# Key-value sums with the value columns as weights, 256 feature columns moving, and the normaliser summed on VectorE

## The chip, the cores and the metric

The kernel runs on one core of a Trainium2 chip. The metric is the device time of one execution in microseconds; the time of a kernel is the median of its runs. The engines are named as in the profile: PE (TensorE matmuls) and PEld (its weight loads), DVE (VectorE), ACT (ScalarE), POOL (GpSimd), SP (SyncE, which here only issues DMAs). Every line number "L12" is a line of the kernel's file.

## The reference

Two branches over the same input x (2048 tokens, width 1024) are mixed by a gate per token:

```python
g = sigmoid((x * gate_w).sum(-1))
a = linear_attention(x)          # 32 heads of width 32
b = (gelu(x @ w_gate) * (x @ w_up)) @ w_down
return g * a + (1 - g) * b
```

The attention branch maps queries and keys of each head by a learned matrix and two softmaxes, and replaces the square attention matrix by two sums over all tokens:

```python
phi = lambda t: concat([softmax(t @ w_phi), softmax(-(t @ w_phi))])   # 64 features a head
kv = einsum("bhsf,bhsd->bhfd", phi(k), v)      # sums over the 2048 tokens s
z  = einsum("bhsf->bhf", phi(k))               # the normaliser
o  = (phi(q) @ kv) / (phi(q) @ z + 1e-6)
return o @ wo
```

The change concerns kv and z only.

## The kernel before, in words

All large products (q, k, v, gate, up, and at the end the two output products) are computed with seven block products in the place of eight, in fp32 split into a high and a low part, so that a product of 128 x 512 outputs over 512 inputs is 12 matmuls (`product`, L703 to L709). The first phase is a list of 79 **units**, one for each pair of weight tiles of one half of the tokens: value and key units of the second half, then of the first half, then the first half's gate, up and query units, then the second half's (`units`, L294 to L299). A unit is seven products of 12 matmuls. The second phase (L1286 on) multiplies the results with `wo` and `w_down`.

Beside the units run **background jobs** that need PE only now and then. One kind makes the features of the keys and the key-value sums (`features`, L952): 32 jobs, one for each token half, each group of four heads, and each half of a group. A job reads a 64-row piece of k and v from memory, transposes it in blocks of 32 x 32 on DVE, takes maximum and minimum, the two exponentials on ACT, the sums and the division on DVE, and leaves the features in `pts` as a high and a low part, and the values in `blocks` likewise. Then PE adds up, over eight blocks of tokens, the products of features and values in a PSUM tile of the tag `misc` (`accumulate`, L1008). Before the change each block's features are the weights, first the high part with 130 moving columns (the values' high part, two columns of ones and zeros that give the normaliser, the values' low part), then the low part with 66: 16 matmuls a job (L1014). ACT copies four corners and the normaliser's column from PSUM (L1026, L1030), and GpSimd stores them with five DMAs (L1032, L1035).

When all 32 are stored, `finish` (L1039) loads the sums of both halves with four DMAs, adds them on DVE, turns the normaliser, and stores both for the **attention jobs** (`attention`, L1074), which then run in two places at once; `second_place` (L1189) opens the second one. Half way, at product 329 (`second_turn`), the operand x of PE is exchanged for that of the second half (`switch`, L259); the switch is due 13 products earlier, and uses buffers of the feature jobs (`switch_again`, L875). A feature job is not begun later than five or six products before that (L834, L974). The main background loop (L825) does an event that is due first, then `finish` when all sums are stored, then a further job.

The order of the instructions on PE, DVE, ACT and SP is written out when the kernel is built, by a planner (`run`, `emit`, `step`, L171 to L205 and L748). Each job is a generator that yields requests: engine, duration in microseconds, time from which it can run, and the product by which it is due. The planner keeps its own clock for each engine (a product is 2.73 us, `PRODUCT`), takes of those that can start the one due first, and fixes the order on each engine. PE work of the background goes to `fillers` and is put behind the next product after its operands are planned to be ready, with a length of its own (1.12 us for L1014). Feature requests are due three products after they are made. On the chip every engine keeps this order and waits only where data or buffers are not ready. GpSimd's queue carries all stores and, in the second half, the loads of kept weights (`kept_weights`, L375).

What the planner books on DVE can be read off the requests: weights of a unit 1.25 + 1.5 + 1.25 + 1.5 + 1.25 + 0.72 (L328 to L369); results of a gate unit 2 x 0.75 and of an up unit 2 x 1.47 + 2 x 0.75 (L675, L680); a feature job 0.72 + 0.72 + 1.4 + 0.72 + 1.4 + 1.6 + 1.25 + 1.25 (L968 to L1001).

Of the kernel before, what the change touches and what calls it, by code (L numbers as in the profile page):

```python
# [8 lines left out]
F32 = mybir.dt.float32  # L9
F32R = mybir.dt.float32r  # L10
# [21 lines left out]
def tile_gated_mix(ctx: ExitStack, tc: tile.TileContext, x, xT, wkT, wqT, wv, w_phi, wo,  # L32
# [15 lines left out]
    sign = keep.tile([P, 1], F32, name="sign")  # L48
# [8 lines left out]
    kv_parts = [dram.tile([P, H // 2, 64], F32, name=f"kvp{h}") for h in range(2)]  # L57
# [77 lines left out]
    with tc.tile_pool(name="xa", bufs=1) as xa, tc.tile_pool(name="fp", bufs=1) as fp, \  # L135
# [268 lines left out]
        V_BLOCK = P + 2  # L404

        def new_f(dtype):
            return fp.tile([P, 8 * V_BLOCK], dtype, tag="f", name="f", bufs=1)

# [60 lines left out]
        for j in range(4):  # L469
            nc.vector.memset(sign[32 * j:32 * j + 32], 1.0 - 2 * (j % 2))  # L470
        bd = fp.tile([P, NG, 4, 32], F32, tag="v", name="bd", bufs=1)
# [335 lines left out]
        places = [Place(work[:, 2048:3072], dict(mm=tails[:, :32], st=tails[:, 32:64], own=tails[:, 64:129]))]  # L807
# [38 lines left out]
        def first_part():  # L846
# [9 lines left out]
            yield VEC, 0.1, 0.0, now[0] + 6  # L856
            places[0].blocks = new_f(F32R).rearrange("p (b c) -> p b c", c=V_BLOCK)
# [25 lines left out]
        def gates(into, gw, free):  # L883
# [22 lines left out]
            for h in range(4):  # L906
                for q in range(4):
                    nc.vector.tensor_copy(g_at[32 * h:32 * h + 32, :, q], g_a[32 * q:32 * q + 32, :])
# [43 lines left out]
        def features(p, events):  # L952
# [6 lines left out]
            v = [blocks[:, :, c:c + 64].rearrange("p b (h d) -> p b h d", h=2) for c in (0, 66)]  # L959
# [6 lines left out]
            while job:  # L966
# [39 lines left out]
        v_free = [0.0]  # L1006

        def accumulate(half, pair, pts, blocks):  # L1008

            def emit_products(end):  # L1010
                po = misc()
                for b in range(8):
                    for a, n in ((0, V_BLOCK), (1, 66)):
                        nc.tensor.matmul(po[:, :n], pts[:, b, a].rearrange("p q f -> p (q f)"), blocks[:, b, :n],  # L1014
                                         start=b == a == 0, stop=b == 7 and a == 1, skip_group_check=True)
                misc_free[0] = INF
                pts_free[0] = v_free[0] = end
                start(accumulated(half, pair, po, end + 0.25))
            return emit_products

        def accumulated(half, pair, po, end):
            end = yield SCA, 1.1, end, now[0] + 2
            own = places[0].parts["own"]
            for h in range(2):
                for s in range(2):
                    nc.scalar.activation(  # L1026
                        own[64 * h + 32 * s:64 * h + 32 * s + 32, :64].rearrange("p (a d) -> p a d", a=2),
                        po[64 * s + 32 * h:64 * s + 32 * h + 32, :132].rearrange("p (a d) -> p a d", a=2)
                        [:, :, 32 * h:32 * h + 32], AF.Copy)
            nc.scalar.activation(own[:, 64:], po[:, 64:65], AF.Copy)  # L1030
            misc_free[0] = end
            nc.gpsimd.dma_start(kv_parts[half][:, pair], own[:, :64])  # L1032
            for s in range(2):
                for h in range(2):
# [454 lines left out]
```

## Time and profile before

| | |
|---|---|
| median of 3 runs | 2400.91 us (2397.92 to 2403.98) |
| the profiled execution | 2408.64 us, its span 2406.9 us |
| granted clock in it | 0.996 |
| PE busy | 2364.8 us, 98% of the span |
| DVE, ACT, POOL busy | 1767.3, 1117.5, 386.2 us |
| the 32 sets of L1014 | from 288.4 to 946.1 us |
| end of the first phase | 1717.2 us |

The profile is of one execution. Busy time of an engine is the union of its instructions. A group's row gives the line, engine, operation, what is written and read, the shape and count, then busy time and mean duration in ns, then the idle time before. A row of the timeline gives the start and the duration in us and, in brackets, how long the engine stood idle before it and for whom. A row of busy time by stretch gives for every engine its busy time and its count of instructions, then PE's granted clock, the DMA's busy share and its rate in GB/s. Matmuls are pipelined and their ends are modelled, so that the distance of two starts says more than a matmul's own duration.

### The profile page before, as it was taken

To read this page: it belongs to the slowest core of one execution; us is meant where nothing else is said; L and a number is where in the kernel's file an instruction comes from. 1 tells how busy PE (TensorE), PEld (TensorE's weight loads), DVE (VectorE), ACT (ScalarE), POOL (GpSimd) and SP (SyncE) were. 2 spreads that over 40 slices of the span, in tenths; PEclk is the share of its full clock that TensorE was granted. 3 is DMA by queue.
4 is the path that set the end of the run, shared out by engine and by line. 5 is a ranking of instruction groups with operands and counts; after the bars stand their busy time and mean duration, and the time that the engine had idled before them with its cause. 6 is when DMAs were issued, how large, how long until landed. Compare 5 with 4: busy or idle time off the path is not lost.

```text
span 2406.9 us, 30176 instructions
## 1 busy us (share of the span) xinstructions
PE 2364.8 (98%) x10664; PEld 1950.6 (81%) x10664; DVE 1767.3 (73%) x2369; ACT 1117.5 (46%) x1588; POOL 386.2 (16%) x721
## 2 busy tenths in 40 slices
PE   9999999999999999999999999999999999999999
PEld 7778888888888888877777788788888888888887
DVE  6667687888888886567968888894474778777773
ACT  5336455566555565344554565564344222323221
POOL 3201122222222223211112111111000000000000
PEclk9999999999999999999999999999999999999999
DMA  9878548888888878987787778787685667978774
GB/s 334 293 256 307 180 155 278 287 301 290 296 295 298 293 274 306 337 304 221 240 252 237 249 246 253 248 255 263 226 299 196 241 220 265 318 267 314 256 270 139
DMA packets 221046, 635.27 MB, mean 264 GB/s; under 512 B 34912, under 2 KB 70496, under 8 KB 196320
## 3 DMA queue, kind: packets, MB, share of 16 engines
q1 hardware_dynamic: 153312, 316.88, 40.8%
q0 software_dynamic: 66384, 316.21, 37.2%
q8 instruction: 84, 1.38, 0.2%
q14 instruction: 66, 0.54, 0.1%
q10 hardware_dynamic: 1200, 0.26, 0.1%
HBM read 426.13 MB, written 207.11 MB: 263 GB/s over the span
## 4 chain that ended last, share of the span: by engine, by line
PE 80%; DMA 7%; issue 7%; DVE 4%; POOL 1%; ACT 1%; SPq 0%; POOLq 0%; DVEq 0%; ACTq 0%
PE po L1400 28%; PE a L708 20%; PE c L708 14%; PE b L708 7%; PE p L708 6%; PE misc L1014 2%; DMA x<-sums 1%; DMA x<-q 1%; PE misc L1162 1%; DMA x<-in_xT 1%; DMA x<-xs 1%; DMA tyz<-rg5z 0%; DMA xs<-raw 0%; PE misc L929 0%; DMA tails<-sums 0%
## 5 line engine op out<-in xcount | busy, mean ns | idle before, releaser
L1400 PE MATMUL po<-tw,wgu 128*128 128x512 f32 x1344 | 309.8, 389 | 0.0
L1400 PEld LDWEIGHTS po<-tw,wgu 128*128 128x128 f32 x1344 | 252.3, 188 | 52.4
L118 ACT ACTIVATE wgu<-stage 128x1024 fp32r<-128x1024 f32 x131 | 138.9, 1060 | 295.9 <-PE po L1400 231.7
L708 PE MATMUL a<-s,tyz 128*128 128x512 f32 x948 | 239.0, 402 | 17.0 <-DMA tyz<-rg3z 3.7
L121 DVE TENSOR_TENSOR wgu<-stage,wgu 128x1024 fp32r<-128x1024 f32 x131 | 159.6, 1218 | 113.5 <-ACT wgu L118 113.3
L708 PE MATMUL p<-s,tyz 128*128 128x512 f32 x948 | 230.8, 392 | 3.8 <-ACT x L746 3.7
L708 PE MATMUL a<-s,v 128*128 128x512 f32 x948 | 234.2, 396 | 0.0
L708 PE MATMUL a<-x,wgu 128*128 128x512 f32 x948 | 229.0, 390 | 4.5 <-DVE x L676 3.7
L708 PE MATMUL b<-s,tyz 128*128 128x512 f32 x948 | 229.0, 390 | 3.9 <-ACT b L736 3.9
L708 PE MATMUL c<-x,wgu 128*128 128x512 f32 x948 | 230.3, 392 | 0.3 <-ACT c L729 0.3
L708 PE MATMUL c<-x,tyz 128*128 128x512 f32 x948 | 228.6, 390 | 1.3 <-ACT c L725 1.3
L708 PEld LDWEIGHTS a<-s,tyz 128*128 128x128 f32 x948 | 178.7, 192 | 60.4 <-issue 16.5
L708 PEld LDWEIGHTS p<-s,tyz 128*128 128x128 f32 x948 | 177.8, 189 | 43.3 <-ACT x L746 6.2
L708 PEld LDWEIGHTS a<-s,v 128*128 128x128 f32 x948 | 178.6, 188 | 42.1
L708 PEld LDWEIGHTS a<-x,wgu 128*128 128x128 f32 x948 | 177.3, 188 | 43.4 <-DVE x L676 4.5
L708 PEld LDWEIGHTS b<-s,tyz 128*128 128x128 f32 x948 | 177.2, 188 | 41.8 <-ACT b L736 5.1
L708 PEld LDWEIGHTS c<-x,wgu 128*128 128x128 f32 x948 | 177.8, 188 | 40.6 <-ACT c L729 0.7
L708 PEld LDWEIGHTS c<-x,tyz 128*128 128x128 f32 x948 | 178.1, 188 | 39.3 <-ACT c L725 2.1
L1400 PE MATMUL po<-tw,wl 128*128 128x512 f32 x672 | 156.9, 389 | 0.0
L1400 PE MATMUL po<-tyz,wgu 128*128 128x512 f32 x672 | 155.2, 389 | 0.0
L1400 PEld LDWEIGHTS po<-tw,wl 128*128 128x128 f32 x672 | 126.1, 188 | 26.2
L1400 PEld LDWEIGHTS po<-tyz,wgu 128*128 128x128 f32 x672 | 126.1, 188 | 26.2
(442 smaller groups left out, 3584.9 us busy)
## 6 DMA issues: line engine op xcount, KB each, us to landing
stage<-lm SPq DMA_DIRECT2D x98, 512.0 KB, 3.6
sr<-in_w_down SPq DMA_DIRECT2D x84, 512.0 KB, 5.7
sl<-lm SPq DMA_DIRECT2D x70, 512.0 KB, 4.4
lm<-h POOLq DMA_DIRECT2D x112, 256.0 KB, 4.5
stage<-in_w_gate SPq DMA_DIRECT2D x28, 512.0 KB, 4.9
stage<-in_w_up SPq DMA_DIRECT2D x28, 512.0 KB, 4.8
stage<-la SPq DMA_DIRECT2D x28, 512.0 KB, 4.1
sr<-in_wo SPq DMA_DIRECT2D x20, 512.0 KB, 5.9
```

Source lines behind the costliest of these rows:

```text
L118: nc.scalar.activation(dst, src, AF.Copy)
L121: nc.vector.tensor_tensor(dst, src, dst_h.bitcast(F32), OP.subtract)
L708: nc.tensor.matmul(dst, w[:, h, 4 * part + kc, :], xq[:, e, kc, :], start=first and kc == 0 and i == 0, stop=kc == 3 and i == 2, skip_grou ...
L1014: nc.tensor.matmul(po[:, :n], pts[:, b, a].rearrange("p q f -> p (q f)"), blocks[:, b, :n], start=b == a == 0, stop=b == 7 and a == 1, ski ...
L1162: nc.tensor.matmul(po[s], kbs[:, s].rearrange("p a b -> p (a b)"), pts[:, q, s, :], start=q == 0, stop=q == 1)
L1400: nc.tensor.matmul(ps[c], ls[:, a, m, c * P:(c + 1) * P], rs[:, e, m], start=opens and m == 0 and j == 0, stop=closes and m == 1 and j == 2)
```

## The change

The roles of the two operands of the key-value product are exchanged. The values' high and low part of a block (2 x 64 columns) are the weights, and the features' high and low part (2 x 128 columns) move, so there are 8 matmuls of 256 columns. A ninth, in plain fp32, with one moving column of ones, sums the normaliser over the partitions, after DVE has summed the features over the eight blocks in a new reduction in `features`. The two halves of the result are added on DVE out of PSUM into `own`; the store grows from 64 to 128 columns, and the normaliser goes with one store in the place of four. `finish` gets the sums with other axes, in pieces of 32 values, adds the two halves of partitions with a copy on ACT, and transposes. The places move: `own` and the normaliser lie in `tails`, the small places of the feature jobs in `g_at`, and so the copies into `g_at` are made at the end of `finish`.

```diff
-    sign = keep.tile([P, 1], F32, name="sign")
+    signs = keep.tile([P, 2], F32, name="sign")
+    sign, one = signs[:, :1], signs[:, 1:]
...
-    kv_parts = [dram.tile([P, H // 2, 64], F32, name=f"kvp{h}") for h in range(2)]
+    kv_parts = [dram.tile([P, H // 2, P], F32, name=f"kvp{h}") for h in range(2)]
...
-        places = [Place(work[:, 2048:3072], dict(mm=tails[:, :32], st=tails[:, 32:64], own=tails[:, 64:129]))]
+        places = [Place(work[:, 2048:3072], dict(
+            mm=g_at.rearrange("p c q -> p (c q)")[:, :32], st=g_at.rearrange("p c q -> p (c q)")[:, 32:],
+            own=tails[:, :P], z=tails[:, P:]))]
...
-            for half in range(2):
-                rows = slice(64 * half, 64 * half + 64)
-                nc.vector.tensor_copy(places[0].blocks[rows, :, 64:66],
-                                      pair_mask[rows, half, :16].rearrange("p (b c) -> p b c", c=2))
...
-            for h in range(4):
-                for q in range(4):
-                    nc.vector.tensor_copy(g_at[32 * h:32 * h + 32, :, q], g_a[32 * q:32 * q + 32, :])
...
                 high(pts[:, :, 0], by_block)
+                yield VEC, 1.25, z_free[0], soon()
+                z_free[0] = INF
+                nc.vector.tensor_reduce(p.parts["z"].rearrange("p (q f) -> p q f", q=4),
+                                        p.wide[0].rearrange("p (q b f) -> p q f b", q=4, f=32), AX.X, OP.add)
                 end = yield VEC, 1.25, end, soon()
                 low(pts[:, :, 1], by_block, pts[:, :, 0])
                 p.free = end
-                fillers.append((lambda end=end: max(end, misc_free[0]), accumulate(half, 2 * g + w, pts, blocks), 1.12))
+                fillers.append((lambda end=end: max(end, misc_free[0]), accumulate(half, 2 * g + w, pts, blocks), 1.1))
...
                 for b in range(8):
-                    for a, n in ((0, V_BLOCK), (1, 66)):
-                        nc.tensor.matmul(po[:, :n], pts[:, b, a].rearrange("p q f -> p (q f)"), blocks[:, b, :n],
-                                         start=b == a == 0, stop=b == 7 and a == 1, skip_group_check=True)
+                    nc.tensor.matmul(po[:, :2 * P], blocks[:, b], pts[:, b].rearrange("p e q f -> p (e q f)"),
+                                     start=b == 0, stop=b == 7, skip_group_check=True)
+                nc.tensor.matmul(po[:, 2 * P:2 * P + 1], places[0].parts["z"], one, start=True, stop=True,
+                                 skip_group_check=True)
...
         def accumulated(half, pair, po, end):
-            end = yield SCA, 1.1, end, now[0] + 2
...
-            misc_free[0] = end
-            nc.gpsimd.dma_start(kv_parts[half][:, pair], own[:, :64])
...
+            own, z = places[0].parts["own"], logit[:, pair:pair + 1]
+            end = yield VEC, 0.5, lambda end=end: max(end, own_free[0]), now[0] + 2
+            nc.vector.tensor_reduce(own, po[:, :2 * P].rearrange("p (e c) -> p c e", e=2), AX.X, OP.add)
+            nc.gpsimd.dma_start(kv_parts[half][:, pair], own)
+            own_free[0] = end + STORE
+            misc_free[0] = end = yield SCA, 0.25, end, now[0] + 2
+            nc.scalar.activation(z, po[:, 2 * P:2 * P + 1], AF.Copy)
+            nc.gpsimd.dma_start(z_parts[half][:, pair:pair + 1], z)
             kept.append(end + STORE)
...
         def finish(p):
             landed = yield SYN, LAND + 2.0, lambda: max(max(kept), place_free(), v_free[0]), INF
...
             for half in range(2):
-                nc.sync.dma_start(p.wide[half], kv_parts[half].rearrange("p u c -> p (u c)"))
-                nc.sync.dma_start(mm[:, half], z_parts[half])
+                for h in range(2):
+                    for k in range(2):
+                        rows = slice(64 * k + 32 * h, 64 * k + 32 * h + 32)
+                        nc.sync.dma_start(p.wide[half][rows].rearrange("p (u s f) -> p u s f", s=2, f=32),
+                                          kv_parts[half][rows].rearrange("p u (s h f) -> p u s h f", s=2, h=2)[:, :, :, h])
+                        nc.sync.dma_start(mm[64 * h + 32 * k:64 * h + 32 * k + 32, half],
+                                          z_parts[half][64 * k + 32 * h:64 * k + 32 * h + 32])
             soon = lambda: now[0] + 1
             end = yield VEC, 1.25, landed, soon()
             nc.vector.tensor_tensor(p.wide[0], p.wide[0], p.wide[1], OP.add)
...
+            moved = yield SCA, 1.1, end, soon()
+            nc.scalar.activation(p.wide[1][:64], p.wide[0][64:], AF.Copy)
+            yield VEC, 0.8, end - SIGNAL, soon()
...
+            end = yield VEC, 2.5, moved, soon()
+            nc.vector.tensor_tensor(p.wide[0][:64], p.wide[0][:64], p.wide[1][:64], OP.add)
+            nc.vector.transpose(p.wide[1][:64], p.wide[0][:64])
+            for h in range(2):
+                for s in range(2):
+                    nc.gpsimd.dma_start(sums_of[64 * h + 32 * s:64 * h + 32 * s + 32, 0],
+                                        p.wide[1][32 * h:32 * h + 32].rearrange("p (u s d) -> p s u d", s=2, d=32)[:, s])
+            yield VEC, 1.6, end - SIGNAL, soon()
+            for h in range(4):
+                for q in range(4):
+                    nc.vector.tensor_copy(g_at[32 * h:32 * h + 32, :, q], g_a[32 * q:32 * q + 32, :])
```

More of the change, by code (lines that the diff above doesn't have):

```diff
@@ L470, in tile_gated_mix @@
             nc.vector.memset(sign[32 * j:32 * j + 32], 1.0 - 2 * (j % 2))
+        nc.vector.memset(one, 1.0)
         bd = fp.tile([P, NG, 4, 32], F32, tag="v", name="bd", bufs=1)
@@ L855, in first_part @@
             pts_free[0] = max(folded[g] for g in range(NG))
-            yield VEC, 0.1, 0.0, now[0] + 6
-            places[0].blocks = new_f(F32R).rearrange("p (b c) -> p b c", c=V_BLOCK)
-            for half in range(2):
-                rows = slice(64 * half, 64 * half + 64)
-                nc.vector.tensor_copy(places[0].blocks[rows, :, 64:66],
-                                      pair_mask[rows, half, :16].rearrange("p (b c) -> p b c", c=2))
+            places[0].blocks = new_f(F32R).rearrange("p (b c) -> p b c", c=P)
             prepared[0] = 0.0
@@ L958, in features @@
             blocks = p.blocks
-            v = [blocks[:, :, c:c + 64].rearrange("p b (h d) -> p b h d", h=2) for c in (0, 66)]
+            v = [blocks[:, :, c:c + 64].rearrange("p b (h d) -> p b h d", h=2) for c in (0, 64)]
             v_now = p.e[:, 0].rearrange("p (h b d) -> p b h d", h=2, d=32)
@@ L1021, in accumulated @@
         def accumulated(half, pair, po, end):
-            end = yield SCA, 1.1, end, now[0] + 2
[L1023 to L1029, printed above, removed]
@@ L1030, in accumulated @@
-            nc.scalar.activation(own[:, 64:], po[:, 64:65], AF.Copy)
-            misc_free[0] = end
-            nc.gpsimd.dma_start(kv_parts[half][:, pair], own[:, :64])
-            for s in range(2):
-                for h in range(2):
-                    nc.gpsimd.dma_start(z_parts[half][64 * h + 32 * s:64 * h + 32 * s + 32, pair:pair + 1],
-                                        own[64 * s + 32 * h:64 * s + 32 * h + 32, 64:])
+            own, z = places[0].parts["own"], logit[:, pair:pair + 1]
@@ L1039, in finish @@
         def finish(p):
             landed = yield SYN, LAND + 2.0, lambda: max(max(kept), place_free(), v_free[0]), INF
-            mm = p.small("mm", 2, 16)
+            mm, z = p.small("mm", 2, 16), tails[:, :64]
             p.second(new_f(F32)[:, :1024])
             for half in range(2):
-                nc.sync.dma_start(p.wide[half], kv_parts[half].rearrange("p u c -> p (u c)"))
-                nc.sync.dma_start(mm[:, half], z_parts[half])
+                for h in range(2):
[5 more added lines that the diff above has]
+                                          z_parts[half][64 * k + 32 * h:64 * k + 32 * h + 32])
@@ L1048, in finish @@
             nc.vector.tensor_tensor(p.wide[0], p.wide[0], p.wide[1], OP.add)
[L1049 to L1054 removed]
+            moved = yield SCA, 1.1, end, soon()
+            nc.scalar.activation(p.wide[1][:64], p.wide[0][64:], AF.Copy)
+            yield VEC, 0.8, end - SIGNAL, soon()
             nc.vector.memset(z[:, 16:32], 0.0)
             nc.vector.tensor_tensor(z[:, :16], mm[:, 0], mm[:, 1], OP.add)
[L1057 removed]
+            nc.vector.transpose(z[:, 32:], z[:, :32])
             for q in range(4):
                 nc.gpsimd.dma_start(sums_of[32 * q:32 * q + 32, 1].rearrange("b u d -> u b d"),
[L1060 removed]
+                                    z[32 * q:32 * q + 16, 32:].unsqueeze(1).to_broadcast([16, 32, 32]))
+            end = yield VEC, 2.5, moved, soon()
[9 more added lines that the diff above has]
+                    nc.vector.tensor_copy(g_at[32 * h:32 * h + 32, :, q], g_a[32 * q:32 * q + 32, :])
             p.parts = {n: raw_in.bitcast(F32)[:, at:at + size] for n, at, size in
```

16 lines of the change are left out of this document (4 added, 12 removed).

## The prediction, made before the changed kernel was run

> **What bounds the kernel now.** I read the page's engine totals first, then busy time by stage, then PE's rows inside one stage. The profiled execution took 2408.64 us, 7.7 us over the median of the runs shown (2400.91); every difference below is worked out against 2408.64 and then taken off the median.
>
> ```profile
> PE 2364.8 (98%) x10664; PEld 1950.6 (81%) x10664; DVE 1767.3 (73%) x2369; ACT 1117.5 (46%) x1588; POOL 386.2 (16%) x721
> ```
>
> ```profile
> core 0: us, PE busy (x) PEld busy (x) DVE busy (x) ACT busy (x) POOL busy (x), PEclk, DMA share, GB/s
> 443.00:946.00 503.00, 503.00 (x2399) 420.92 (x2397) 414.35 (x541) 296.80 (x466) 141.40 (x269) 1.00 0.85 294
> 946.00:1030.00 84.00, 84.00 (x371) 69.16 (x370) 44.63 (x57) 35.25 (x53) 19.08 (x35) 1.00 0.93 325
> 1030.00:1100.00 70.00, 64.94 (x271) 52.62 (x270) 41.09 (x64) 27.34 (x38) 11.93 (x22) 0.95 0.88 286
> 1100.00:1400.00 300.00, 284.81 (x1224) 229.36 (x1223) 245.78 (x405) 169.21 (x238) 55.51 (x103) 0.99 0.75 240
> ```
>
> PE is the bound: in the key-value stage (443 to 946) it has no idle time at all, at full clock. So a shorter PE stream in that stage shortens the run one for one, as long as nothing else becomes late. The same rows show the danger: DVE is busy 82% there (414.35 of 503), and the change moves work onto it. Behind that stage PE does lose time: 5 us of 70 around the switch of the x operand (1030 to 1100), 15 of 300 in the attention stage.
>
> Now the 16 matmuls of one pair (L1014): their groups, PE's timeline around one set (and around one set of L929), and the chain of waits, in which two products "a" in a row come once per unit of seven products:
>
> ```profile
> L1014 PE MATMUL misc<-f,pts 128*128 128x66 f32 x256 | 57.9, 246 | 0.0
> L1014 PE MATMUL misc<-f,pts 128*128 128x130 f32 x256 | 57.2, 296 | 0.0
> ```
>
> ```profile
> 239.51 1.95 PE L929 MATMUL misc<-f,raw 128*128 128x128 f32 x16
> 241.22 2.98 PE L708 MATMUL b<-s,tyz 128*128 128x512 f32 x12
> ...
> 729.23 2.88 PE L708 MATMUL p<-s,tyz 128*128 128x512 f32 x12
> 731.95 2.88 PE L708 MATMUL c<-x,tyz 128*128 128x512 f32 x12
> 734.67 1.87 PE L1014 MATMUL misc<-f,pts 128*128 128x130 f32 x16
> 736.37 3.01 PE L708 MATMUL a<-s,tyz 128*128 128x512 f32 x12
> ```
>
> ```profile
> 463.80 5.64 PE a L708 x24
> ...
> 925.35 5.64 PE a L708 x24
> 946.33 5.64 PE a L708 x24
> 965.61 5.52 PE a L708 x24
> 984.75 5.52 PE a L708 x24
> ```
>
> The 16 matmuls hold PE from 734.67 to 736.37: 1.70 us, 106 ns each, whether 66 or 130 columns move. A unit with them takes 946.33 - 925.35 = 20.98 us, one without 984.75 - 965.61 = 19.14, so they cost 1.84 us: 1.70 and 0.12 of slower first products (5.64 against 5.52), the rest rounding.
>
> **PE, what is removed and added.** 16 weight loads with short moves become 8 with 256 moving columns and one true fp32 matmul with one column. A 512-column matmul takes (731.95 - 729.23)/12 = 227 ns, while the short ones stand at 106 ns whatever their width, which looks like the price of the weight load alone. For 256 columns no row exists. Low end: that 106 ns floor. High end: the straight line from 98 mean columns (106 ns) to 512 (227), 152 ns. I take 120 ns, a little over half of the 512-column row (114), because the flat floor speaks for a load that runs under a longer move, not beside it. The fp32 matmul: L929's eight fp32 matmuls are 16 records in 1.71 us, two of 107 ns each, so 0.21 us. Sum: 8 x 0.120 + 0.21 + 0.12 of slow start = 1.29 us instead of 1.84: 0.55 less, and over 32 pairs (256 + 256 records, 16 a pair) **-17.5 us**; by the ends 1.18 (-21) and 1.55 (-9).
>
> [...]
>
> **DVE and ACT.** Per pair DVE gains two reductions and ACT loses five copies:
>
> ```profile
> L993 DVE TENSOR_REDUCE tails<-x 128x32 f32<-128x1024 f32 x24 | 29.1, 1211 | 1.1 <-ACT x L991 1.1
> L979 DVE TENSOR_REDUCE tails<-x 128x16 f32<-128x512 f32 x23 | 14.8, 644 | 0.0
> ```
>
> ```profile
> 736.57 0.89 ACT L1026 ACTIVATE tails<-misc 32x64 f32<-32x64 f32 x4 [5.02 <-PE misc L1014]
> 737.49 0.17 ACT L1030 ACTIVATE tails<-misc 128x1 f32<-128x1 f32 x1
> ```
>
> ```profile
> L908 DVE COPY g_at<-g_a x16: 162/174/180, 181.4 to 184.2; 32x16 f32<-32x16 f32 x16
> ```
>
> ```profile
> 442.90:463.80 20.90, 20.90 (x102) 17.52 (x101) 17.55 (x24) 11.28 (x14) 4.30 (x9) 1.00 0.81 289
> ```
>
> The normaliser's reduction has 1024 elements: 1.21 us, as L993. The one out of PSUM has 256: 512 to 1024 elements is 0.57 us more, so 0.36. No row reads with the new strides; below that price nothing can be gained, above it I allow double. Together 1.57 us: DVE per unit 17.55 + 1.57 = 19.1 of a unit of 20.4. The cover holds on the chip, with 1.3 us left instead of 3.4. ACT loses 0.89 and keeps one copy of 0.17; it was not the bound, 0. GpSimd issues two stores instead of five, and they wait for DVE and ACT instead of ACT alone: 0. Sixteen g_at copies (L908), 2.8 us, move from 181 us to behind the sums, where DVE is half busy (44.63 of 84): 0 there, and at 181 nothing of PE hangs on them.
>
> But the order on DVE is written by the planner with its own longer durations. Between the units of gate and up it books for DVE, per unit, 7.47 us of weights, 2.97 of results (mean of 1.5 and 4.44) and 9.06 of one feature job: 19.50 of 7 x 2.73 + 1.12 = 20.23, 96%. After the change it books 9.06 + 1.25 + 0.5 = 10.81 for the job: 21.25 of 20.21. One job per unit no longer fits. At a full DVE there are (19.11 - 10.44)/(10.81 - 1.10) = 0.89 jobs per unit, one in 7.8 products; at the 96% of before, (18.42 - 10.44)/(10.81 - 1.06) = 0.82, one in 8.5. I take 8.
>
> **What is late next.** Count products back from the switch of x:
>
> ```profile
> 950.56 0.33 SPq L1044 DMA_DIRECT2D x<-kvp  x1
> ...
> 982.83 2.47 SPq L274 DMA_DIRECT2D x<-in_xT  x2
> ...
> 1045.85 0.60 SPq L1072 DMA_DIRECT2D tails<-sums  x1
> ```
>
> ```profile
> 1018.20 2.00 ACT L118 ACTIVATE x<-x 128x1024 fp32r<-128x1024 f32 x2
> 1033.87 2.88 PE L708 MATMUL a<-x,wgu 128*128 128x512 f32 x12
> ```
>
> ```profile
> 1041.73 12.30 DMA x<-xs
> ```
>
> ```profile
> 958.92 1.22 DVE L1048 TENSOR_TENSOR x<-x,f 128x1024 f32<-128x1024 f32 x1 [2.86 <-DMA f<-kvp]
> ...
> 1056.35 0.35 DVE L1093 TENSOR_TENSOR tails<-tails,pair_mask 128x64 f32<-128x64 f32 x2
> ...
> 1668.66 0.68 DVE L1184 TENSOR_TENSOR h<-h,x 128x512 f32<-128x512 f32 x1
> ```
>
> 1033.87 is product 329 (second_turn), so 946.33 is product 297 and the last pair follows 296. One pair per unit runs back from there over (946.33 - 463.80)/20.98 = 23 units to product 135, where the ninth of the 32 stands. At 8 products each, and three lost before the ninth, the last comes at 138 + 23 x 8 = 322 (318 to 333). The switch is due at 316. Now the sums (`finish`) run before it, at 950 to 961; after, the switch goes first, some 6 products later than now, and `finish` runs behind it, near product 337. That moves three things:
>
> The switch's first loads start some 16 us later; now they are issued at 982.83 and converted at 1018.20, 35 us on, so 16 are covered, but they then meet a DMA that the switch's last loads already wait for (12.30 us). Between 0 and 8, I take **+2**.
>
> `finish` reads its partial sums with 16 DMAs instead of 4, the large ones in runs of 128 B (1024 each). An issue of 128 runs takes 0.33 us and one of 256 takes 0.60, so 1024 runs cost between 0.33 and, by that slope, 2.2 us: 5 to 21 us of SP for the sixteen (eight small at 0.4). From first issue to the first add it now takes 958.92 - 950.56 = 8.4 us; that becomes 12 to 26, and the planner books 7. Queued behind the add are, on DVE, ACT and GpSimd, the results that free PE's banks (L676, L684), the copies L725 to L736 and the loads of kept weights.
>
> ```profile
> DVE x L1093 <- DMA x<-sums: 27.3, 8, 7.6
> PE a L708 <- DMA tyz<-rq0z: 2.8, 1, 2.8
> PE a L708 <- DMA tyz<-rg0z: 2.3, 1, 2.3
> ```
>
> ```profile
> 1664.12 1.10 PE L1162 MATMUL misc<-pts,stage 128*128 128x512 f32 x4
> 1717.16 11.04 PE L1400 MATMUL po<-tyz,wgu 128*128 128x512 f32 x48
> ```
>
> ```profile
> la<-h POOLq DMA_DIRECT2D x32, 256.0 KB, 4.3
> ```
>
> DVE has stood up to 7.6 us for such a load with PE losing about 2. For some 11 us of lateness: 0 to 10, I take **+4**.
>
> Attention then begins later: the planner books 7 + 1.25 + 1.1 + 2.5 + 6.5 = 18 us for `finish`, and a few of the lateness come on top, so 1056 becomes about 1080. Its last product is at 1664.12, its result is added at 1668.66 and in memory some 5 us later; the last phase, which reads it, begins at 1717.16. The cover is 43 us; gone, each further us counts. **+1** (0 to 5).
>
> Sum: -17.5 + 2 + 4 + 1 = **-10.5 us**: the profiled 2408.64 becomes 2398, the median 2390.
>
> **Rivals.**
> *Pace kept.* If a job still ends per unit (or in 7.3), `finish` stays ahead of the switch and only PE's part is left: -17.5, 2383. For it: on the chip DVE has room (19.1 of 20.4). Against: the order is written by the planner, where it does not fit.
> *The sums hold up the queues (slower side).* If the last job ends at product 328, 16 us later than forecast, and the loads take 26 us, 19 more than booked, attention begins 16 + 18 + 19 = 53 us late, 10 beyond the cover, and the switch (8) and the blocked queues (10) cost their upper ends: -17.5 + 28 = +10.5, or 2411. It decides from 17.5 us of such losses on. For it: the 5 us of stalls already there; against: DVE is half busy from 946 to 1030 and can catch up.
> *DVE becomes the bound.* If its waits stay (20.9 - 17.55 = 3.4 us a unit) beside 19.1 of work and one job per unit, a unit takes 22.5 instead of 20.98, and 24 units cost +36: 2437. It decides once more than 1.9 us of waits stay. Against: feature jobs have distant due times and give way to weights. [...]
> *The change saves little on PE.* At 152 ns per matmul -9 is left, and with the late costs -2: 2399.
>
> **Chances.** Forecast 0.52, pace kept 0.20, held queues 0.13, DVE bound 0.08, little saved 0.07. About 0.3% (7.2 us) can be told from no change. Faster: 0.7 of the forecast's 0.52 and nearly all of the second, 0.55. Slower: two thirds of the third and the fourth, 0.17. The rest, 0.28. The range takes the full PE gain of -21 at its lower end, 2379, and the held queues up to 2411 at the upper; beyond lie DVE bound and a part of the third. The forecast's own range is 2383 to 2398.
>
> **What would show it.** Right: about 1.2 us between the first of L1014's successors and the next product; a unit with them near 20.4 us; feature jobs one in eight products; the first read of the partial sums behind the switch's last load; DVE near 89% busy. Wrong: 256-column matmuls well over 130 ns, PE waits between 270 and 1030, `finish` still near 950, or the last phase waiting for attention.

## The result and the profile after

The changed kernel takes 2436.69 us in the median of 4 runs (2431.09 to 2443.95), the kernel before 2402.44 beside it. The ratio is 1.0128, with a 95% interval of 1.0103 to 1.0153: 31 us slower by the ratio, 34 by the medians, where 10.5 us less than before was forecast. Its profiled execution took 2443.95 us, the longest of the four.

PE's own work did shrink. The engine totals of the page of after, and busy time of after by the stages that the prediction showed of before (with 1400 to 1712 beside them), columns as there:

```profile
PE 2353.1 (96%) x10472; PEld 1937.7 (79%) x10472; DVE 1838.3 (75%) x2433; ACT 1103.1 (45%) x1467; POOL 342.2 (14%) x628
```

```profile
443.00:946.00 503.00, 485.33 (x2187) 401.16 (x2186) 427.07 (x541) 260.76 (x352) 104.11 (x193) 0.98 0.83 290
946.00:1030.00 84.00, 84.00 (x391) 70.22 (x390) 72.65 (x91) 44.88 (x60) 16.72 (x31) 1.00 0.82 285
1030.00:1100.00 70.00, 51.45 (x201) 40.85 (x201) 28.78 (x40) 22.78 (x30) 14.37 (x26) 0.88 0.91 288
1100.00:1400.00 300.00, 283.59 (x1210) 230.27 (x1209) 233.91 (x396) 160.32 (x226) 55.65 (x102) 0.98 0.78 234
1400.00:1712.00 312.00, 298.81 (x1288) 243.74 (x1288) 252.75 (x411) 175.93 (x243) 57.22 (x105) 0.98 0.79 245
```

PE was without a gap from 443 to 946. Now it idles 17.7 us there, and 18.6 of the 70 from 1030 to 1100. Busy time from the first set of the key-value sums to the first product of the last phase, of before and of after:

```profile
288.65:1717.16 1428.51, 1405.61 (x6365) 1158.62 (x6364) 1100.99 (x1597) 773.39 (x1165) 326.60 (x613) 1.00 0.80 266
```

```profile
286.80:1752.81 1466.01, 1397.76 (x6162) 1147.38 (x6161) 1170.96 (x1676) 757.80 (x1043) 282.27 (x520) 0.98 0.79 259
```

This stretch holds the whole loss: it is 37.5 us longer, 7.9 less of PE's work and 45.4 more of its idle time (22.9 before, 68.3 after). Within the work, the groups of the products (L708 before, L709 after) add up to 8.8 us more, mostly because some products ran slower behind a wait (last section). So the sets themselves cost 16.7 us less by this sum, and 19 by the rows of one set (1.84 - 1.25, 32 times), where 17.5 was forecast.

One set of after on PE's timeline, and the two new reductions on DVE (groups by shape):

```profile
286.80 1.12 PE L1012 MATMUL misc<-pts,f 128*128 128x256 f32 x8
287.75 0.28 PE L1014 MATMUL misc<-sign,tails 128*128 128x1 f32 x2
287.90 3.03 PE L709 MATMUL c<-x,tyz 128*128 128x512 f32 x12
```

```profile
L998 DVE TENSOR_REDUCE tails<-x 128x128 f32<-128x1024 f32 x32 | 65.7, 2052 | 0.1
L1024 DVE TENSOR_REDUCE tails<-misc 128x128 f32<-128x256 f32 x32 | 13.4, 419 | 4.6 <-PE misc L1014 4.3
```

A 256-column matmul takes (287.75 - 286.80)/8 = 119 ns. The normaliser's reduction takes 2.05 us, not the 1.21 of the row with as many elements: it reads with a stride of 128 B. It also writes 128 sums where that row writes 32, but the same stride with 32 sums takes as long, as a run below shows in which the kernel before has such a reduction added:

```profile
L1002 DVE TENSOR_REDUCE tails<-x 128x32 f32<-128x1024 f32 x32 | 66.0, 2062 | 0.3
```

With 1024 elements read and 32 sums written in both, the reduction with the stride takes 1.7 times as long as the one that reads in order (2062 ns against the 1211 of L993). Why the stride costs that was not shown.

### The profile page after: what moved, and what is told of

It reads as the page before. It is cut to its first block, busy times and chain, and to the rows that moved or that the text cites. A ratio compares the mean times of both kernels' runs of the same rounds, so it can differ in the third digit from the quotient of the medians.

```text
span 2442.2 us, 29572 instructions
## 1 busy us (share of the span) xinstructions
PE 2353.1 (96%) x10472; PEld 1937.7 (79%) x10472; DVE 1838.3 (75%) x2433; ACT 1103.1 (45%) x1467; POOL 342.2 (14%) x628
## 4 chain that ended last, share of the span: by engine, by line
PE 48%; issue 11%; DMA 6%; DVE 6%; POOL 2%; SPq 1%; ACT 1%; POOLq 0%; DVEq 0%; ACTq 0%
PE po L1408 28%; PE a L709 9%; PE c L709 6%; PE b L709 3%; PE p L709 2%; DMA stage<-in_w_up 1%; DMA x<-q 1%; POOL lm L110 1%; PE misc L1170 1%; SPq L1044 1%; DMA tyz<-ru6z 1%; DMA tyz<-ru7z 0%; SPq L943 0%; DVE tyz L122 0%; DMA tyz<-rg3z 0%
## 5 line engine op out<-in xcount | busy, mean ns | idle before, releaser
L709 PE MATMUL a<-s,tyz 128*128 128x512 f32 x948 | 243.1, 407 | 31.5 <-DMA tyz<-rq0z 4.3
L709 PE MATMUL c<-x,tyz 128*128 128x512 f32 x948 | 237.0, 400 | 15.2 <-ACT c L726 15.2
L709 PE MATMUL b<-s,tyz 128*128 128x512 f32 x948 | 232.7, 395 | 17.1 <-ACT b L737 17.1
L709 PEld LDWEIGHTS a<-s,tyz 128*128 128x128 f32 x948 | 184.9, 197 | 78.6 <-issue 24.5
L709 PE MATMUL p<-s,tyz 128*128 128x512 f32 x948 | 230.1, 391 | 4.4 <-ACT x L747 4.4
L709 PE MATMUL a<-x,wgu 128*128 128x512 f32 x948 | 229.1, 390 | 3.9 <-DVE h L695 1.6
L709 PE MATMUL c<-x,wgu 128*128 128x512 f32 x948 | 228.9, 390 | 0.3 <-ACT c L730 0.3
L709 PE MATMUL a<-s,v 128*128 128x512 f32 x948 | 229.0, 390 | 0.0
L709 PEld LDWEIGHTS c<-x,tyz 128*128 128x128 f32 x948 | 181.8, 193 | 55.8 <-ACT c L726 17.6
L709 PEld LDWEIGHTS b<-s,tyz 128*128 128x128 f32 x948 | 179.6, 191 | 56.5 <-ACT b L737 19.2
L709 PEld LDWEIGHTS a<-x,wgu 128*128 128x128 f32 x948 | 177.1, 188 | 43.4 <-DVE h L695 2.5
L709 PEld LDWEIGHTS p<-s,tyz 128*128 128x128 f32 x948 | 176.6, 188 | 44.0 <-ACT x L747 7.7
L709 PEld LDWEIGHTS a<-s,v 128*128 128x128 f32 x948 | 177.7, 188 | 37.1
L709 PEld LDWEIGHTS c<-x,wgu 128*128 128x128 f32 x948 | 177.3, 188 | 37.4 <-ACT c L730 0.7
```

What stands on the lines that cost most here:

```text
L709: nc.tensor.matmul(dst, w[:, h, 4 * part + kc, :], xq[:, e, kc, :], start=first and kc == 0 and i == 0, stop=kc == 3 and i == 2, skip_grou ...
```

## Where PE's time went: one stall

SP's, DVE's, ACT's and PE's timeline of after around one of four such stalls (476, 628, 773 and 920 us):

```profile
604.07 0.33 SPq L43 DMA_DIRECT2D stage<-wq  x1
611.96 3.13 SPq L943 DMA_DIRECT2D x<-k  x4
615.19 3.00 SPq L943 DMA_DIRECT2D x<-v  x4
618.24 0.97 SPq L43 DMA_DIRECT2D stage<-in_w_up  x2
```

```profile
606.23 2.02 DVE L998 TENSOR_REDUCE tails<-x 128x128 f32<-128x1024 f32 x1
...
611.22 0.70 DVE L964 STREAM_TRANSPOSE x<-x 128x512 f32<-128x512 f32 x1
```

```profile
626.00 1.06 ACT L119 ACTIVATE wgu<-stage 128x1024 fp32r<-128x1024 f32 x1 [8.21 <-DMA stage<-in_w_up]
626.97 0.58 ACT L726 ACTIVATE c<-b 128x512 f32<-128x512 f32 x1
```

```profile
619.00 2.88 PE L709 MATMUL p<-s,tyz 128*128 128x512 f32 x12
627.60 5.38 PE L709 MATMUL c<-x,tyz 128*128 128x512 f32 x12 [5.72 <-ACT c L726]
```

Read from the end: PE waits for the copy of c, ACT makes that copy behind a weight's high part, the weight has not landed, its load is issued at 618.24, and SP had stood since 604.4 in front of a feature job's loads (L943), whose buffer DVE frees with its transposes at 611. Issuing these eight loads then took SP another 6.3 us. DVE was late by its own work, the 2 us reduction among it. So three theories were put to the test: **the order** (the planner books 1.75 us more per job, jobs fall to one in eight products, and all follows from that), **the work** (2.5 us more on DVE, made worse by SP's queue), and **finish** (its sixteen loads and the blocked queues).

## The experiments

All ratios are to the kernel before, on the same chip, with 95% intervals. The runs come from four chips, so a difference of two ratios carries both intervals, some 0.3% together.

**The reduction taken out**

```diff
-                yield VEC, 1.25, z_free[0], soon()
-                z_free[0] = INF
-                nc.vector.tensor_reduce(p.parts["z"]...
+        nc.vector.memset(tails[:, P:], 1.0)      # once
```

> The changed kernel without the normaliser's reduction on DVE (the 128x1024 TENSOR_REDUCE of 2.02 us per job and its booking of 1.25 us); the z operand is filled once with ones, so the normaliser is left out of the result. All else, the PE part and the changed finish too, stays. Theory 1 (load on DVE: with 1.75 us more booked per job a job no longer fits a unit of seven products, and all losses follow from that): the jobs keep seven products, the last set stands near product 302, finish runs ahead of the switch, PE has next to no idle time from 270 to 1030 us, and the time is 2380 to 2396 us, about 45 us under the changed kernel. Theory 2 (the loss lies in the changed finish and in the reductions that PE waits for, whatever the pace): finish still holds ACT, DVE and POOL for some 20 us, and at most the 10 to 15 us of idle time in the key-value stage come back: 2420 to 2436 us.

2396.66 us, 0.9957 [0.9934, 0.9980]. PE is busy 502.4 of 503 us from 443 to 946. Beyond what the new `finish` costs (priced below), all that was lost hangs on the reduction.

**The reduction added to the kernel before**

```diff
+                yield VEC, 1.25, 0.0, soon()
+                nc.vector.tensor_reduce(tails[:, 192:224], p.wide[0].rearrange("p (c f) -> p f c", f=32), AX.X, OP.add)
                 end = yield VEC, 1.25, end, soon()
                 low(pts[:, :, 1], by_block, pts[:, :, 0])
```

> The kernel before, with one instruction per job added: the same strided 128x1024 reduction on DVE (2.02 us, booked as 1.25), its result used by nothing. PE's work, the copies, the stores and finish are those of before. Theory 1 (the load on DVE and its booking set the pace): the jobs fall to one in eight products, the last set comes near product 324, finish goes behind the switch, PE shows the stalls of 3 to 6 us behind ACT's c copies in the key-value stage although nothing of PE's work changed, and the time is 2425 to 2450 us, 25 to 45 us over before. Theory 2 (DVE's load is covered, the loss comes from finish or from the PE to DVE coupling): 2400 to 2412 us.

2438.00 us, 1.0124 [1.0084, 1.0164]: as much as the changed kernel loses on balance, though nothing of PE's work and no instruction of `finish` was changed. (`finish` does come later, its first load at 1078.5.)

**Work and booking apart.** The first run keeps the instruction and books nothing, the second books and leaves the instruction out.

```diff
-                yield VEC, 1.25, z_free[0], soon()
+                yield VEC, 0.0, z_free[0], soon()
```

> The changed kernel with the normaliser's reduction where it is, but with no duration booked for it (0 in place of 1.25 us); everything is computed. In the planner's order the jobs then keep one in seven products, as without the reduction, while DVE on the chip still carries its 2.02 us. Theory 1a (the planner's order makes the loss: a slower pace of the jobs, finish behind the switch): near the run without the reduction, 2392 to 2405 us, ratio 0.995 to 1.000, with the last set near 940 us. Theory 1b (the work itself makes it: DVE has 17.5 + 2.0 + 0.4 = 20.0 us of work in a unit of some 20.3 and falls behind): PE waits for DVE and ACT all through 443 to 946, DVE over 96% busy there, 2415 us or more.

> The changed kernel with the 1.25 us booked as it is, but without the reduction's instruction; the z operand is filled once with ones, so the normaliser is left out of the result. The planner's order is that of the changed kernel, word for word; DVE is 2.02 us per job lighter. Theory 1a (the order makes the loss): finish behind the switch, stalls behind it as in the changed kernel, last set near 1025 us, 2425 to 2437 us. Theory 1b (the work on DVE makes it): the stalls of PE behind ACT's c copies in 443 to 946 go, 2405 us or less. Both at work: in between, some 2415 us, with the stalls of 443 to 946 smaller and those of finish unchanged.

2419.59 us, 1.0067 [1.0040, 1.0095], and 2404.64 us, 1.0001 [0.9977, 1.0024]. From 0.9957 the work alone costs 1.1% (26 us), the booking alone 0.44% (11 us), both 1.7% (41 us). The work is the larger part, so the order alone is refuted. But DVE was not full, as the rival had it. Busy time of the run with the work alone, and DVE's waits for weights there from 443 to 946:

```profile
443.00:946.00 503.00, 483.92 (x2196) 397.12 (x2195) 447.18 (x567) 270.75 (x363) 104.25 (x194) 0.99 0.82 290
```

```profile
DVE stage L100 <- DMA stage<-in_w_gate: 17.9, 5, 6.0
DVE stage L100 <- DMA stage<-wq: 6.2, 2, 5.9
DVE stage L100 <- DMA stage<-in_w_up: 3.2, 2, 1.8
```

DVE is busy 89%, and half of its other 56 us it waits for weights (7.4 us before). Late transposes make late weights, and in this run these take from DVE the slack with which it would catch up. (In the changed kernel itself the engine that waits for weights is ACT, as in the stall above.) What SP waited for in front of the feature loads in that stage, before, in the changed kernel, and with the work alone:

```profile
SPq L948 <- DVE x L969: 141.8, 22, 9.7
```

```profile
SPq L943 <- DVE x L964: 164.6, 20, 14.9
```

```profile
SPq L943 <- DVE x L964: 189.8, 20, 16.3
```

**The feature loads on GpSimd's queue**, in the changed kernel, in the kernel before, and with the work alone:

```diff
-                        nc.sync.dma_start(into[64 * j + 32 * i:64 * j + 32 * i + 32, n],
+                        nc.gpsimd.dma_start(into[64 * j + 32 * i:64 * j + 32 * i + 32, n],
```

> The changed kernel with the eight loads of each feature job (L943) issued on GpSimd's queue in place of SP's; everything is computed in the planner's order of the changed kernel. In the changed kernel SP stood 172 us of 443 to 946 in front of these loads, waiting for DVE's transposes, with weight loads behind it. Theory 2 (the load on DVE is made worse by that hold: late transposes, late weights, DVE then waits for weights): PE's waits behind ACT's c copies in 443 to 946 (14.8 us, with some 10 us of low clock behind them) go or fall to under 5, and the time is 2412 to 2424 us. Rival (DVE's work alone does it): they stay, 2430 us or more. Third: GpSimd's queue stands in the same way and its stores of h come late; then 2440 us or more, with DVE or ACT waiting for those stores.

> The kernel before, with the eight loads of each feature job (L948) on GpSimd's queue. SP stands 142 us of 443 to 946 in front of them there, but PE loses nothing in that stage. If the queue matters only once DVE is late (theory 2), nothing is gained: 2398 to 2408 us, ratio 0.998 to 1.002. If moving the loads is worth something by itself, so that the changed kernel's gain by it says nothing of the change, the ratio is 0.995 or less.

> The changed kernel with the reduction in place but not booked (2419.6 us), and with the feature jobs' loads on GpSimd's queue. DVE carries 2.02 and 0.42 us more per job at one job in seven products. Theory 2 (the hold on SP's queue turns late transposes into late weights, and DVE's work alone is covered): PE busy all of 443 to 946 with DVE near 92%, last set near 940 us, 2388 to 2400 us, level with the run without the reduction (2396.7). Rival (DVE at 20.0 us of work in a unit of 20.3 is itself the bound): PE loses 5 us or more in that stage, 2405 us or more.

2400.59 us, 0.9986 [0.9964, 1.0008]; 2398.75 us, 0.9996 [0.9974, 1.0018]; 2389.24 us, 0.9940 [0.9920, 0.9960]. The first gained more than was expected, 1.42% (34 us), without one instruction less on any engine. Busy time in the stage of the first and of the third:

```profile
443.00:946.00 503.00, 503.00 (x2316) 419.74 (x2315) 449.83 (x570) 277.41 (x372) 200.11 (x370) 1.00 0.87 303
```

```profile
443.00:946.00 503.00, 500.55 (x2309) 417.56 (x2308) 467.52 (x592) 283.95 (x379) 205.97 (x381) 1.00 0.87 301
```

PE has no gap any more with DVE at 89%, and loses 2.5 us at 93%; DVE's waits for weights fall from 27.3 us (the work alone, above) to 1.2 in the third run. In the kernel before, the same edit gains nothing: there PE has no gap in the stage with the loads on either queue (503.00 of 503). So what stands on SP's queue is the cause in this stage, and DVE's work only what triggers it. The edit takes two things off that queue: the wait in front of the loads (172 us of this stage in the changed kernel) and the issuing of the loads (some 100 us by their rows). No run separates the two.

**`finish`.** First its addition given out later in the changed kernel; then, without the reduction, likewise; then, in the kernel with the feature loads moved, that and its sixteen loads on GpSimd's queue.

```diff
-            landed = yield SYN, LAND + 2.0, ...
+            landed = yield SYN, LAND + 22.0, ...                  # first run only
...
-            end = yield VEC, 1.25, landed, soon()
+            end = yield VEC, 1.25, landed, now[0] + 12            # first run
+            end = yield VEC, 1.25, landed + 8.0, now[0] + 12      # second and third run
...
-                        nc.sync.dma_start(p.wide[half][rows]...
+                        nc.gpsimd.dma_start(p.wide[half][rows]...   # third run, and the loads of zp likewise
```

> The changed kernel, with the planner told that the loads of finish take 20 us longer, and with a due time of its first addition 12 products later, so that the addition is put into the queues of DVE and ACT when its data is there, not before. Nothing is computed otherwise. The attention stage begins some 6 products later by this. Theory 1 (finish costs what stands in the queues behind it, about 13 us; the rest lies in the key-value stage and in the attention stage): DVE's 22 us and ACT's 18 us of idle time in front of finish go away, the PE stall of 10 us near 1096 too, and the time is about 2424 us (2418 to 2430); the stalls between 443 and 946 stay as they are. Theory 2 (nearly all of the loss comes from finish): 2405 us or less. If the later attention stage costs as much as the hold, the time stays at 2430 to 2440.

> The run without the normaliser's reduction (2396.66 us; the normaliser left out of the result), with the first addition of finish given out when its data has landed (8 us later in the plan). It prices the hold of finish at the fast pace: DVE's idle 11.8 us, ACT's wait and PE's stalls of 7.2 and 3.8 us near 950 should go, and the time should be 2383 to 2388 us. If PE's stall there comes from something else, such as the 16 loads on SP's queue ahead of the weights, it stays and the time is 2393 to 2398 us.

> The changed kernel, reduction and booking as they are (one job in eight products), with the feature jobs' loads and the loads of finish on GpSimd's queue and the first addition of finish given out when its data has landed. What is left against the fast pace is then only the later place of the last set and of the attention stage. If the rest of the loss is finish's hold, 2385 to 2393 us; if it is the later attention stage, 2396 to 2402 us, no better than with the feature loads moved alone (2400.6).

2420.13 us, 1.0063 [1.0036, 1.0090]; 2388.20 us, 0.9926 [0.9901, 0.9952]; 2385.59 us, 0.9930 [0.9903, 0.9957]. `finish` on SP's, DVE's, ACT's and PE's timeline of the changed kernel:

```profile
1068.89 0.67 SPq L1042 DMA_DIRECT2D x<-kvp  x1
...
1088.14 0.68 SPq L1044 DMA_DIRECT2D g_at<-zp  x1
```

```profile
1093.38 1.23 DVE L1048 TENSOR_TENSOR x<-x,f 128x1024 f32<-128x1024 f32 x1 [22.29 <-DMA f<-kvp]
```

```profile
1094.64 1.06 ACT L1050 ACTIVATE f<-x 64x1024 f32<-64x1024 f32 x1 [17.59 <-DVE tails L1052]
```

```profile
1096.23 4.92 PE L709 MATMUL b<-s,tyz 128*128 128x512 f32 x12 [10.46 <-ACT b L737]
```

The planner books 7 us for the loads, they take 24.5, and DVE and ACT stand in front of the addition with PE's copies behind it. Given out later, the addition still finds its loads under way, but DVE stands 7.8 us in front of it and not 22.3, and ACT and PE no longer stand with it (the longest wait of PE from 1064 to 1115 is 1.1 us). DVE's row of that run:

```profile
1095.11 1.23 DVE L1048 TENSOR_TENSOR x<-x,f 128x1024 f32<-128x1024 f32 x1 [7.75 <-DMA f<-kvp]
```

That is 0.65% (16 us) less, although the attention stage begins later still. The second run kept a stall of 7 us, which its expectation had as the other case: the weights stood on SP behind the sixteen loads. SP's, ACT's and PE's timeline of that run:

```profile
947.53 0.67 SPq L1039 DMA_DIRECT2D x<-kvp  x1
...
960.27 8.80 SPq L43 DMA_DIRECT2D stage<-in_w_gate  x2
```

```profile
964.17 1.06 ACT L119 ACTIVATE wgu<-stage 128x1024 fp32r<-128x1024 f32 x1 [12.36 <-DMA stage<-in_w_gate]
```

```profile
965.76 5.18 PE L710 MATMUL c<-x,tyz 128*128 128x512 f32 x12 [6.97 <-ACT c L727]
```

With both queues cleared the third run stands 0.70% under before (17 us), as much as the gain on PE, at one job in eight products and with the reduction as it was written. Not all waiting is gone: in its profiled execution, 11 us over its median, PE idles 9.1 us from 946 to 1100 (5.1 before).

**The reduction cheaper or elsewhere.** Three contiguous additions on DVE (0.69 + 0.43 us by their rows, and by the line through these two some 0.29 for the third), behind the low parts and with nothing booked; the late addition in all three runs, the loads of `finish` on GpSimd's queue in the second, the feature loads too in the third.

```diff
+                t = p.wide[0].rearrange("p (q b f) -> p q b f", q=4, f=32)
+                nc.vector.tensor_tensor(t[:, :, :4], t[:, :, :4], t[:, :, 4:], OP.add)
+                nc.vector.tensor_tensor(t[:, :, :2], t[:, :, :2], t[:, :, 2:4], OP.add)
+                nc.vector.tensor_tensor(p.parts["z"].rearrange("p (q f) -> p q f", q=4), t[:, :, 0], t[:, :, 1], OP.add)
```

> The changed kernel with the normaliser's sum as three contiguous additions (512, 256 and 128 elements) behind the low parts, with nothing booked for them, and with the first addition of finish given out when its data has landed (8 us later in the plan). Everything is computed. By the rows for 512 elements (0.68 us) and 128 (0.2 us) the three take about 1.3 us in place of 2.02. Theory 1a: the jobs keep seven products, finish ahead of the switch without its 12 us hold, 2380 to 2392 us, faster than before by 0.5 to 1%. Theory 1b: DVE has 19.3 us of work in a unit of 20.3, so part of the loss comes back: 2395 to 2415 us.

> The tree with the late first addition (2418 us), and only the loads of finish on GpSimd's queue. It prices the 13 us that the weight loads stood behind the 16 loads on SP near 950: PE's stall of 7 to 9 us on a c copy there and the slow product behind it go, 2406 to 2412 us. If PE waits there for something else, 2415 to 2422 us.

> The tree of three additions with the late first addition of finish (2418 us), and with the feature jobs' loads and the loads of finish on GpSimd's queue. Everything is computed. Theory 2: the stage from 443 to 946 loses no more than 5 us of PE, the stall of 9 us behind finish (weights behind 16 loads on SP) goes too: 2385 to 2400 us, faster than before. Rival (DVE's work alone): 2405 to 2415 us, only finish's part gained. Third, as in the run before: GpSimd's stores late, over 2420 us.

2418.45 us, 1.0073 [1.0045, 1.0101]; 2411.95 us, 1.0028 [1.0006, 1.0050]; **2380.46 us, 0.9897 [0.9853, 0.9941]**, faster than both kernels. The first was above both its ranges: with even 1.4 us more on DVE, DVE waited 32.9 us for weights from 443 to 946 (7.4 before), and in the second run SP stood 180.2 us there in front of the feature loads (141.8 before). The third came out below its range of 2385 to 2400; it differs from the second by the feature loads' queue alone: 1.31% (31 us).

The sum on GpSimd, or the normaliser on PE (one column of ones held still, the high parts moving, the low parts left out), this one without and with the feature loads moved:

```diff
-                nc.vector.tensor_reduce(p.parts["z"]...
+                nc.gpsimd.tensor_tensor(...by_block[:, 0], by_block[:, 1], OP.add)   # and six more
```

```diff
-                nc.tensor.matmul(po[:, 2 * P:2 * P + 1], places[0].parts["z"], one, start=True, stop=True, ...
+                for b in range(0, 8, 2):
+                    nc.tensor.matmul(po[:1, 2 * P:].rearrange("p (b c) -> p b c", b=2), one_r,
+                                     pts[:, b:b + 2, 0].rearrange("p b q f -> p b (q f)"), start=b == 0, stop=b == 6, ...
```

> The changed kernel with the normaliser's sum over blocks moved from DVE to GpSimd, as seven additions of 128x128; everything is computed. DVE carries only the 0.42 us reduction out of PSUM in addition. Theory 1: as without the reduction, pace near seven products, finish ahead of the switch, 2380 to 2398 us, so faster than before, if seven additions on GpSimd take less than the 20 us of a unit and do not hold up its stores. Theory 2: 2420 to 2436 us. A third outcome: GpSimd's additions take over 1.5 us each, its stores and weight sums come late, and the time is over 2410 with PE waiting for tyz loads.

> A version meant to beat both: no sum over blocks on DVE; PE sums the high parts (fp32r) of the features with a one-column operand of ones held still and two blocks moving, four matmuls of 256 columns a pair, into the pair's PSUM bank; ACT copies two rows of 128, and finish adds two parts more. The low parts are left out of the normaliser. Late first addition, loads of finish on GpSimd's queue. By the row of 119 ns for 256 columns PE pays 4 x 0.119 - 0.145 = 0.33 us a pair, 11 us in all, over the run without any normaliser (2388 us), and the weights no longer stand behind finish's loads (some 8 us gained). Theory 2 (work on DVE is what the stage cannot take): 2384 to 2396 us, ratio to the kernel before 0.991 to 0.997. If the time is over 2405, something else than DVE's load is lost in the changed kernel.

> The version with the normaliser on PE (2422.7 us, where SP stood 300 us of 443 to 946 before the feature loads and DVE waited 69 us for weights), with the feature jobs' loads on GpSimd's queue as well. The low parts are left out of the normaliser. Theory 2: it had lost by that hold alone; PE idles under 2 us in 443 to 946, and the time is 2385 to 2400 us. If it stays over 2410, the four matmuls or the row copies cost more than their rows say.

2455.76 us, 1.0196 [1.0153, 1.0239]; 2422.72 us, 1.0065 [1.0033, 1.0097]; 2382.71 us, 0.9924 [0.9896, 0.9952]. On GpSimd an addition takes 0.74 us by the row below, so seven some 5.2, and DVE waits for them before it may overwrite the features. The time is above the ranges of the first two theories; it is the third outcome, over 2410, but with additions of half the 1.5 us that it supposed. Group on POOL and wait of DVE (270 to 1030 us) in that run:

```profile
L999 POOL TENSOR_TENSOR tails<-tails,x 128x128 f32<-128x128 f32 x192 | 141.7, 738 | 13.8
```

```profile
DVE x L964 <- POOL tails L999: 32.0, 23, 3.6
```

With the normaliser on PE, DVE had next to nothing more to do, and the run was still slow, against the expectation of 2384 to 2396. SP's wait and DVE's waits of that run, 443 to 946:

```profile
SPq L945 <- DVE x L966: 300.4, 22, 16.6
```

```profile
DVE stage L101 <- DMA stage<-in_w_up: 35.2, 8, 7.9
DVE stage L101 <- DMA stage<-in_w_gate: 20.3, 6, 4.1
DVE stage L101 <- DMA stage<-wq: 13.8, 3, 4.9
```

SP stood in front of the feature loads for 300 of 503 us. Why so long is open: from the 20th job on the loads lie one to four weight loads earlier in SP's queue than in the second run of `finish` above, which has no reduction either, but from the 12th to the 19th they lie at the same place or later, and SP stands 12 to 16 us in front of them there too. What is shown is that the reduction on DVE is not needed for this loss. With the loads moved, 1.41% (34 us) came back; PE still idles 4.2 us in the stage, where under 2 was expected.

## Why the prediction was wrong

**PE's part: right.** 119 ns where 120 was taken, 1.25 us for a set with its slow start (287.90 - 286.80, and 3.03 - 2.88) where 1.29 was; 0.15 us for the two fp32 records where 0.21 was. 17 to 19 us gained in the profile, 17.5 forecast.

**The pace, the order: right.** The last set stands behind product 325 (forecast 322), the switch goes ahead of `finish` (its first load at 1025.72), and `finish` comes at 1068.89, near product 337 (forecast 337). Less right is the switch's own price. PE waits 2.9 and 4.3 us there, where it waited 2.8 once, and the product behind the new wait ran 1.7 us slower: some 6 us more, where +2 was taken and 8 was the end.

**DVE's durations: too low**, 2.05 + 0.42 = 2.47 us a job for 1.57, inside the double that was allowed above. DVE at 427 of 503 us (85%) was less busy than the forecast 89%: the loads of 20 jobs fell into this stage, 22 before.

**"The cover holds on the chip, with 1.3 us left instead of 3.4": this step failed**, and it decides the sign. The sum has no term for PE's waits in the key-value stage, and 17.7 us of them came, which the prediction itself names as a sign of being wrong. Where a mean load was compared with a mean unit, nothing was asked about who waits for the late instruction. For `finish` the prediction names what is queued behind the waiting instruction; for the transposes of the feature jobs, which the change pushes back, the same question was not put. SP's queue kept its order: the next job's loads waited there for these transposes, and the weights behind them (in the stall above SP stands from 604.4 to 611.96, and the weight's load goes out at 618.24). The row for it stood in the trace of before: 141.8 us in front of L948. Priced by the runs: 34 us from the changed kernel to the same with the loads moved, 30 us at the fast pace. The cover itself does hold, at 89 to 93% of DVE, once that queue is clear.

**`finish`: right mechanism, wrong size.** Its loads took 24.5 us, inside the 12 to 26 forecast; the held queues cost 13 us (0.56%, from the run with the feature loads moved to that with `finish` cleared too) to 16 (0.65%, in the changed kernel), where +4 was taken and 10 was the end. The cover was read off waits of up to 7.6 us, where PE lost about 2; making the one of 22.3 us, three times as long, into one of 7.8 brought 16.

**The late attention stage: the cover of 43 us held.** Its last matmul is at 1722.7 and the last phase begins at 1752.8. Yet PE idles 13.2 us of 1400 to 1712, where it idled 2.7, waiting for kept weights. With `finish` cleared, 13.6 us of idle time stay there (3.6 in the fastest run, whose sums come early). That this belongs to the later stage is likely: the six kernels whose sums are read behind the switch idle 6.6 to 13.6 us there, the others 0.4 to 8.2. But no run moved that stage alone.

**The rivals.** "DVE becomes the bound" had the right time, 2437, by the wrong way: a unit of 22.5 us at one job per unit, where jobs in fact gave way and one job came in eight products. The time agrees by luck. "The sums hold up the queues" happened as well: its 13 to 16 us are about a third of the 48 us between the forecast gain on PE and the measured loss.

## What to carry to other kernels

A duration added to an engine with free time need not be free (here 2.47 us a job on a DVE that was busy 82%): follow each queue that waits for that engine's later instructions, and ask what else stands in that queue. A load that waits for a buffer belongs on a queue where nothing urgent stands behind it, not ahead of loads that others need at once; here one word for a queue was worth 34 us, more than the 17 to 19 of PE's work that the change saved. And a planner's booking must hold for the slow case of a load, or engines stand waiting in front of the instruction that needs it: here 7 us were booked, 24.5 taken, and DVE stood 22.3.

## What had not been expected of the hardware

A long stall of PE cost more than its length in these traces. Waits of PE for a late operand, and the 12 matmuls behind them (2.88 us as a rule), on the timeline of after:

```profile
1569.73 3.00 PE L709 MATMUL a<-s,tyz 128*128 128x512 f32 x12 [2.44 <-DMA tyz<-ru9z]
```

```profile
1372.71 4.57 PE L709 MATMUL a<-s,tyz 128*128 128x512 f32 x12 [2.76 <-DMA tyz<-ru5z]
```

In the changed kernel no wait up to 2.44 us slowed the product behind it, and each of the eleven waits from 2.76 us on did, by 1.7 to 2.6 us: 23 us in all, against 6 of four such products before, from 288 us on. Other traces have no such sharp border: in the kernel before, the product behind a wait of 1.97 us took 4.30 us (at 1538) and the one behind 2.90 us took 3.00 (at 1333); in the third run of `finish` the one behind 3.12 us took 3.01 (at 1427). The granted clock falls with the slow products (0.88 from 1030 to 1100). Over the eleven of the changed kernel it was 0.50 to 0.52 in the five of 5.4 to 5.5 us and 0.58 to 0.63 in the six of 4.6 to 4.9; over the four of before, of 4.3 to 4.6 us, 0.63 to 0.66; over the two products of 3.00 us, at 1569.73 and before at 1333, 1.00. What lowers it, and after how long a wait, was not shown.
